# A fused attention and gated-MLP kernel: a persistent row of ones in the key-query tiles of the F32 heads, and a new instruction order

## The chip, the cores and the metric

The kernel runs on one core of one Trainium2 chip. The metric is the device time of one execution in microseconds (us). Before the change it is 783.78 us, the median of three runs (783.1 to 788.05).

## The reference

Attention with a bias from cumulative sums over 8 batches of 8 heads, 576 tokens of 64 dimensions, and behind it a gated MLP that mixes over tokens. Cut to what is computed:

```python
# attention, per batch and head: q, k, v are 576 x 64, s is 576
s_pos = np.maximum(s, 0.0)
cum = np.cumsum(s_pos, axis=-1)
bias = -(cum[:, :, :, None] - cum[:, :, None, :])
scores = np.where(causal, -1e9, q @ k.T / 8 + np.minimum(bias, 0.0))
attn = softmax(scores)                       # 1e-9 is added to the sum
x = (attn @ v).transpose(0, 2, 1, 3)         # 8 x 576 x 512
# MLP, per batch
h = gelu_tanh(x @ w_in)                      # 576 x 1024
u, v = h[..., :512], h[..., 512:]
v_n = (v - mean(v)) / sqrt(var(v) + 1e-6) * g_ln
v_s = einsum('ts,bsd->btd', w_sg, v_n) + b_sg[None, :, None]
out = x + (u * v_s) @ w_out
```

## The kernel before

**Work.** Each of the 64 heads passes three steps: `scores` (q times k with the cumulative sums as one extra row of the contraction, five query tiles `it` of 64 to 576 columns, then a masked minimum on VectorE, DVE below, and an exponential on ScalarE, ACT), `transposes` (twelve 128x128 transposes on TensorE, PE, into tiles `pa`, `pb`, `pd`) and `pv` (the product with v, tiles `xx` and, from head 16 on, `x0`, which the profile calls `x`). Eight heads are a batch, and `ffn` then runs the MLP of that batch while the next batch's heads go on. In the profile its PE groups are `vm`, `um`, `sm` and `om`.

**Precision.** Heads 0 to 11 (`h < NQ`) take q and k in plain F32, and heads 0 to 15 (`h < NP`) take v in plain F32. All later work is split into a high and a low F32R part, two or three matmuls each.

**The F32 heads' tile.** `kt` holds two tiles `kf` of 128 x 2 x 576, used in turn (`kt[h % 2]`). Rows 0 to 63 hold q in plane 0 and k in plane 1. Row 64 is the bias row: ones on the side of q, and head h's scaled cumulative sums, `cf[h]`, on the side of k. Rows 65 to 127 stay zero. The function `load` fills a tile with two transfers from the SP queue: `in_kf`, which in the kernel before brings 65 rows (row 64 with ones in plane 0 and zeros in plane 1), and, for h > 0, `cf[h]` into row 64 of plane 1. The second overwrites bytes of the first, so it waits until the first has landed, and SP issues its transfers strictly in order. Head 0 adds its bias with matmuls of their own (`sc<-cf,wz`).

**Order.** Nothing is issued where the code stands. Every operation is recorded with a key (`nc.key`, a place on the time axis of heads), a table `SHIFT` moves kinds of operations by some heads' time in each of five phases (`PHASE`), and `plan` schedules the recorded graph with the costs of `cost`, a latency per pair of engines plus `MARGIN` ns, and 280 bytes per ns for transfers. What comes out is one fixed sequence for each engine. All instructions therefore have one line in the profile, L418. `nc.gate` makes what is recorded under it start after another instruction has started.

**Start.** PE runs `WARM` matmuls on a constant tile (`wm<-wz`), then the cumulative sums (`cps`), which ACT and DVE bring to `cf`. GpSimd (POOL) clears the two `kf` tiles. The MLP weights arrive as 64-bit floats (`wraw`), and ACT, POOL and DVE turn them into two F32R parts (`wbits`, `wi`, `wo`), in the first 130 us, between the heads' work.

Of the kernel before, what the change touches and what calls it, by code (L numbers as in the profile page):

```python
# [17 lines left out]
B, H, S, D = 8, 8, 576, 64  # L18
# [3 lines left out]
P = 128  # L22
# [22 lines left out]
ORDL = ("v0 u00 v1 v2 u01 u02 v3 v4 u10 u11 s00 u12 u03 s01 s03 u13 s10 "  # L45
        "s02 o00 o01 s11 s12 s13 o03 o02 o11 o13 o10 o12")
CV = 1.4
WARM = 9
FULL = {(128, 192): 300.0, (128, 288): 525.0, (128, 320): 690.0, (128, 448): 830.0, (64, 64): 130.0, (128, 64): 200.0,
        (64, 128): 150.0, (64, 192): 215.0, (64, 256): 290.0}  # L50
NQ = 12
# [17 lines left out]
LATENCY = [[54, 38, 39, 80, 60], [54, 35, 33, 77, 60], [54, 34, 35, 90, 60], [55, 34, 35, 80, 60], [1060] * 5]  # L69
OVERLAP = [0, 93, 75, 25, 0]  # L70
YIELD = {DVE: 95, POOL: 60}
MARGIN = 58.3
ISSUE = 640.0
PHASE = (4.0, 9.0, 13.5, 61.5)
SHIFT = {
    "act activation p__ 128x192 p__": (4.33, 4.33, 4.33, 4.33, 4.33),
    "act activation p__ 128x320 p__": (-5.08, -5.08, -5.08, -5.08, -5.08),
    "act activation p__ 128x576 p__": (-3.57, -3.57, -3.57, -3.57, -3.57),
    "act activation p__ 64x64 p__": (0, 0, -2, 1.33, 0),
# [3 lines left out]
    "act copy k 128x576 raw": (0, 0, 0, 5.05, 0),  # L83
    "act copy pbh 128x256 pt": (6.99, 6.99, 6.99, 6.99, 6.99),
    "act copy pbh 64x128 pt": (0, 0, 0, 6.37, 6.37),
    "act copy pbl 128x128 pt": (2.4, 2.4, 2.4, 2.4, 0),
    "act copy pdh 128x256 pt": (0, 0, 0, -4.2, -4.2),
    "act copy vs 128x384 vr": (0, 0, 0, 1.69, 1.69),
    "act copy wi 128x256 wbits": (1.92, 1.92, 1.92, 0, 0),
# [5 lines left out]
    "dve scalar_tensor_tensor wbits 128x256 wraw": (0, 1.04, 0, 0, 0),  # L95
    "dve tensor_copy pbh 128x512 pt": (2.51, 2.51, 2.51, 2.51, 0),
    "dve tensor_copy pdh 128x256 pt": (0, 0, 0, -0.91, 0),
    "dve tensor_copy rt 10x128 pt": (-4.03, -4.03, -4.03, -4.03, -4.03),
    "dve tensor_scalar wbits 128x256 wbits": (0, 0, 6.16, 6.16, 0),
    "dve tensor_tensor pal 128x512 pt": (0, 0, 0, 3.87, 3.87),  # L100
    "dve tensor_tensor pbl 128x512 pt": (0, 0, 0, 0.91, 0.91),
    "dve tensor_tensor pdl 128x192 pt": (0, 0, 0, -1.48, -1.48),
    "dve tensor_tensor u 128x288 sm": (0, 0, 0, -0.43, -0.43),
    "dve tensor_tensor vm 64x512 vm": (0, 0, -2.45, 0, 0),
    "dve tensor_tensor_reduce p__ 128x192 sc": (-0.99, -0.99, -0.99, -0.99, -0.99),
    "dve tensor_tensor_reduce p__ 128x288 sc": (0, 1.63, 0, 0, 0),
    "dve tensor_tensor_reduce p__ 128x320 sc": (3.92, 3.92, 3.92, 3.92, 3.92),
    "dve tensor_tensor_reduce p__ 64x64 sc": (0, 0, 4.41, -23.41, 0),
# [23 lines left out]
    "pool tensor_scalar p__ 64x64 p__": (2.01, 2.01, 2.01, 2.01, 2.01),  # L132
    "pool tensor_scalar wbits 128x256 wbits": (0, 0, -7.72, 0, 0),
    "pool tensor_tensor gt 128x288 u": (0, 0, 0, 1.88, 1.88),
    "pool tensor_tensor k 128x576 raw": (0, 0, 0.53, 0, 0),
    "pool tensor_tensor wo 128x256 wbits": (0, 0, 19.65, 19.65, 0),
# [3 lines left out]
}  # L140


# [100 lines left out]
class Program:  # L243
# [30 lines left out]
    def cost(self, op):  # L274
        e, name, ins, outs, kw = op["eng"].n, op["name"], op["ins"], op["outs"], op["kw"]
        big = [v for v in ins if v.columns() > 1]
        n = outs[0].columns() if outs else big[0].columns()
# [3 lines left out]
        if e == PE:  # L281
            if name == "group":
                d, load = 2150.0, 54.0
            elif name == "transpose":
                d, load, port = 110.0, 0.84 * ins[0].columns(), 1.0
            else:
                w, m = ins
                load, n = 0.84 * w.columns(), m.columns()
                d = 0.463 * n if m.dtype == F32R else FULL.get((w.columns(), n), 2.0 * n + 60)
        elif e == ACT:  # L290
            f = kw.get("func")
            d = (195 if not any(ps) else 166) + 0.834 * n
            if f == AF.Exp:
                d, gap = 480 + 0.834 * n, -107
            elif n == 512 and f == AF.Copy:
                d = 715
            elif n == 384:
                gap = 115
            elif f == AF.Tanh:
                d += 10  # L300
        elif e == DVE:
            d = 150 + 1.045 * n
            if name == "scalar_tensor_tensor" and n == 512 and any(ps):
                d += 55
            if name == "tensor_tensor_reduce":
                d += 67 if isinstance(kw["scalar"], View) else 7
            elif name == "reciprocal":
                d = 202
            elif name == "bn_stats":
                d, gap = 687, 118  # L310
            elif name == "bn_aggr":
                d = 172
            elif name == "memset":
                d = 60 + 0.8 * n
            elif n > 1 and not ops_ and not any(ps):
                d = 152 + 1.04 * n if len(big) > 1 else 70 + 0.8 * n
                port = d
        elif e == POOL:
            if name == "tensor_tensor":
                d = (560 if kw["op"] == ALU.pow else 193) if n == 1 else 177 + 2.17 * n  # L320
            elif name == "tensor_scalar":
                d = 180 + (1.01 if n == 512 else 0.84) * n if n > 4 else 210
                if kw["op0"] == ALU.max:
                    d = 3.3 * n
            else:
                d = 140 + n
            if n > 4 and ins:
                port = min(d, 265.0) if kw.get("op0") == ALU.max else d
        else:
            v = (outs or big)[0]  # L330
            d, load = v.dims[0][1] * v.columns() * 4 / 280.0, ISSUE
        if e in (ACT, DVE) and any(v.off[1] for v in outs + big if v.columns() > 1):
            load, gap = 20.0, OVERLAP[e] + 25
        return e, d, load, port, gap
# [231 lines left out]
def tile_attn_gmlp(  # L566
# [45 lines left out]
    def load(h):  # L612
        d = heads[h] = {}
        if h < NQ:
            t = kt[h % 2]
            k = d["k"] = t[:, 1, :]
            d["q"] = t.rearrange("p a n -> p (a n)")
            r = D + (h > 0)
            nc.sync.dma_start(out=t[0:r], in_=kf[h, 0:r])
            if h:  # L620
                nc.sync.dma_start(out=k[D:D + 1, :], in_=cf[h:h + 1, :])
        else:
# [21 lines left out]
    for i in range(WARM):  # L644
# [8 lines left out]
    nc.gpsimd.memset(tri.bitcast(F32), 8.0)  # L653
    x = nc.gpsimd.affine_select(out=tri, in_=tri.bitcast(F32), pattern=[[1, S]], base=0, channel_multiplier=-1,
                                compare_op=ALU.is_ge, fill=0.0)
    nc.gate = x
    kt = []
    for i in range(2):
        t = att.tile([P, 2, S], F32, name="kf", tag="k1")
        kt_done = nc.gpsimd.memset(t[64:P].rearrange("p a n -> p (a n)"), 0.0)  # L660
        kt.append(t)
    nc.gate = None
    sp = moe.tile([P, 5, 2, BH], F32R, name="sp", tag="vn", bufs=4)
# [589 lines left out]
def _layout(i):  # L1253
# [5 lines left out]
    tok = (np.array(TOK)[:, None] * REM + np.arange(REM)).ravel()  # L1259
    kq = np.concatenate([k.transpose(0, 2, 1), q.transpose(0, 2, 1)[:, :, tok]], axis=1)  # L1260
    kf = kq[:NQ].reshape(NQ, 2, D, S)[:, ::-1].transpose(0, 2, 1, 3)
    row = np.zeros((NQ, 1, 2, S), q.dtype)
    row[:, :, 0] = 1
    kf = np.concatenate([kf, row], axis=1)
    v6 = np.concatenate([v, v[:, NT * P:], v[:, 0:REM], v[:, 0:REM]], axis=1)
    v6[:NP, NT * P:S] = 0
    v6[:NP, 5 * P + REM:] = 0
# [37 lines left out]
```

## Time and profile before

| what | us |
|---|---|
| median of three runs | 783.78 |
| lowest and highest run | 783.1, 788.05 |
| the profiled execution | 786.85 |
| its span, first to last instruction | 785.1 |
| busy in it: PE, DVE, ACT, POOL | 758.7, 602.5, 561.2, 499.3 |

The prediction reads the profile in views. A row of a list by time gives start, duration, engine, line, operation, output and inputs, and in brackets how long the engine stood idle before it and what ended that. SPq rows are transfers being issued by SP, not their flight. PEclk is the clock that PE was granted, 1.00 being full. In the chain of waits, which follows the last instruction back to what released it, a row gives start, duration and what ran.

### The profile page before, as it was taken

The numbers are of one execution on the slowest core, as the hardware profiler recorded it, in microseconds if no ns is written. First come the engines' busy times: TensorE is split into PE (matmuls) and PEld (weight loads), VectorE is DVE, ScalarE is ACT, GpSimd is POOL, SyncE is SP. The second block draws the span as 40 slices with busy tenths as digits, with TensorE's granted clock in tenths as the row PEclk, the third lists the DMA queues.
The fourth block names the chain that finished last, engine by engine and source line by source line (L and its number), as shares of the span: only waits on it lengthen the run. The fifth ranks groups of instructions, "written<-read, shape, count | busy, mean of one in ns | idle before, by whom it ended". The sixth has DMA issues, their size and how long they took to land.

```text
span 785.1 us, 16981 instructions
## 1 busy us (share of the span) xinstructions
PE 758.7 (97%) x5246; PEld 695.6 (89%) x5246; DVE 602.5 (77%) x1856; ACT 561.2 (71%) x1582; POOL 499.3 (64%) x820
## 2 busy tenths in 40 slices
PE   8998889999999999999999999999999999999998
PEld 6766668899899998999989998999989999899998
DVE  6678679866897769985899768987699858984662
ACT  4867867765888768885888758886688858871340
POOL 6557887774668565685567756684756856654541
PEclk9999999999999999999999999999999999999999
DMA  7547673553535625454344635356254544401101
GB/s 204 144 115 184 186 176 89 125 142 89 136 105 130 176 73 154 117 140 132 106 130 108 179 88 138 109 137 175 72 157 116 138 122 114 109 30 31 52 15 61
DMA packets 74119, 94.24 MB, mean 120 GB/s; under 512 B 29816, under 2 KB 44600, under 8 KB 74028
## 3 DMA queue, kind: packets, MB, share of 16 engines
q1 hardware_dynamic: 74028, 93.15, 44.7%
q8 instruction: 42, 0.69, 0.4%
q14 instruction: 49, 0.40, 0.2%
HBM read 49.38 MB, written 9.90 MB: 75 GB/s over the span
## 4 chain that ended last, share of the span: by engine, by line
PE 69%; DVE 10%; ACT 8%; DMA 4%; POOL 4%; issue 3%; SPq 1%; POOLq 0%; ACTq 0%; DVEq 0%
PE sm L418 12%; PE om L418 12%; PE sc L418 10%; PE vm L418 9%; PE xx L418 9%; PE um L418 9%; PE pt L418 7%; ACT p L418 3%; DVE u L418 1%; DVE p L418 1%; ACT k L418 1%; DVE pbl L418 1%; DVE xr L418 1%; DMA out_t<-ot 1%; DVE vt L418 1%
## 5 line engine op out<-in xcount | busy, mean ns | idle before, releaser
L418 ACT ACTIVATE p<-p,mn 128x192 f32<-128x192 f32 (+4 forms) x320 | 178.3, 558 | 36.3 <-DVE mn L418 34.0
L418 DVE CUSTOM_DVE_ANT_0 p<-sc,mask 128x288 f32<-128x288 f32 (+4 forms) x320 | 124.0, 421 | 9.1 <-PE sc L418 6.9
L418 PE MATMUL sm<-ws,vn 128*128 128x288 f32 x768 | 130.6, 300 | 0.2 <-DVE u L418 0.2
L418 PE MATMUL pt<-ident,p 128*128 128x128 f32 x768 | 120.7, 279 | 6.5 <-ACT p L418 5.0
L418 PE MATMUL om<-gt,wo 128*128 128x288 f32 x768 | 123.6, 299 | 0.0
L418 PE MATMUL um<-xs,wi 128*128 128x288 f32 x768 | 122.0, 301 | 0.0
L418 PE MATMUL vm<-wi,xs 128*128 128x512 f32 (+1 forms) x416 | 114.6, 401 | 0.0
L418 PEld LDWEIGHTS sm<-ws,vn 128*128 128x128 f32 x768 | 110.3, 189 | 1.9 <-DVE u L418 0.6
L418 PEld LDWEIGHTS om<-gt,wo 128*128 128x128 f32 x768 | 108.8, 188 | 1.2
L418 PEld LDWEIGHTS um<-xs,wi 128*128 128x128 f32 x768 | 106.7, 188 | 0.7
L418 PEld LDWEIGHTS pt<-ident,p 128*128 128x128 f32 x768 | 90.8, 141 | 17.0 <-ACT p L418 7.5
L418 PE MATMUL sc<-k 128*128 128x288 f32 (+4 forms) x312 | 87.4, 295 | 2.1 <-DVE vnr L418 0.8
L418 POOL TENSOR_TENSOR k<-raw,k 128x576 fp32r<-128x576 f32 x52 | 74.2, 1427 | 18.9 <-ACT k L418 18.6
L418 PEld LDWEIGHTS vm<-wi,xs 128*128 128x128 f32 (+1 forms) x416 | 73.8, 184 | 13.1
L418 PE MATMUL sc<-k,q 66*128 66x288 f32 (+4 forms) x312 | 80.5, 302 | 0.0
L418 POOL TENSOR_SCALAR p<-p 64x64 f32<-64x64 f32 x128 | 30.8, 240 | 69.1 <-ACT p L418 49.1
L418 DVE SCALAR_TENSOR_TENSOR u<-u,um 128x288 f32<-128x288 f32 x128 | 56.5, 448 | 17.4 <-ACT u L418 15.3
L418 DVE TENSOR_TENSOR pbl<-pt,pbh 128x512 fp32r<-128x512 f32 (+3 forms) x120 | 55.3, 469 | 17.0 <-ACT pbh L418 12.8
L418 POOL TENSOR_TENSOR gt<-u,gt 128x288 fp32r<-128x288 f32 x64 | 51.0, 807 | 22.7 <-ACT gt L418 22.7
L418 PEld LDWEIGHTS sc<-k 128*128 128x128 f32 (+1 forms) x312 | 55.4, 180 | 6.0 <-issue 1.2
L418 ACT ACTIVATION_READ_ACCUMULATOR p<-p,mn 128x1 f32 (+1 forms) x320 | 60.4, 189 | 0.0
L418 POOL TENSOR_TENSOR vs<-vr,vs 128x384 fp32r<-128x384 f32 x48 | 48.7, 1015 | 17.2 <-POOL p L418 8.9
(131 smaller groups left out, 1685.3 us busy)
## 6 DMA issues: line engine op xcount, KB each, us to landing
k<-k SPq DMA_DIRECT2D x156, 144.0 KB
raw<-in_kq SPq DMA_DIRECT2D x52, 288.0 KB
vr<-in_vp SPq DMA_DIRECT2D x48, 192.0 KB
rb<-rd SPq DMA_DIRECT2D x64, 144.0 KB
out_t<-ot SPq DMA_DIRECT2D x64, 144.0 KB
q<-k SPq DMA_DIRECT2D x52, 144.0 KB
wraw<-in_w_in SPq DMA_DIRECT2D x16, 256.0 KB
kf<-in_kf SPq DMA_DIRECT2D x11, 292.5 KB
```

What stands on the lines that cost most here:

```text
L418: real[i] = [getattr(op["eng"].real, name)(*[f(a) for a in args], **{k: f(v) for k, v in kw.items()}).ins for args, kw in calls]
```

## The change

Row 64 of the two tiles is no longer loaded. After the clearing of rows 64 to 127 a second memset writes ones into row 64 of plane 0, once, and `load` brings 64 rows. So the transfer of `cf[h]` shares no byte with the transfer of `in_kf`, and neither waits for the other. Both still wait until the matmuls of head h - 2 have read the tile. The first tile is now cleared by DVE, the second by POOL, and only the second one behind the gate. The host no longer appends the row.

The order is found anew: `SHIFT` is another table, `MARGIN` goes from 58.3 to 54.62 ns, transfers are planned at 235 bytes per ns, and there are ten `wm` matmuls.

```diff
-WARM = 9
+WARM = 10
...
-MARGIN = 58.3
+MARGIN = 54.62
...
-    "act activation p__ 128x192 p__": (4.33, 4.33, 4.33, 4.33, 4.33),
...
+    "act activation p__ 128x192 p__": (0, 0, 3, 3, 3),
...
-            d, load = v.dims[0][1] * v.columns() * 4 / 280.0, ISSUE
+            d, load = v.dims[0][1] * v.columns() * 4 / 235.0, ISSUE
...
-            r = D + (h > 0)
-            nc.sync.dma_start(out=t[0:r], in_=kf[h, 0:r])
+            nc.sync.dma_start(out=t[0:D], in_=kf[h])
             if h:
                 nc.sync.dma_start(out=k[D:D + 1, :], in_=cf[h:h + 1, :])
...
-    nc.gate = x
     kt = []
     for i in range(2):
         t = att.tile([P, 2, S], F32, name="kf", tag="k1")
-        kt_done = nc.gpsimd.memset(t[64:P].rearrange("p a n -> p (a n)"), 0.0)
+        e = (nc.vector, nc.gpsimd)[i]
+        nc.gate = x if i else None
+        kt_done = e.memset(t[64:P].rearrange("p a n -> p (a n)"), 0.0)
+        e.memset(t[64:65, 0, :], 1.0)
         kt.append(t)
...
-    row = np.zeros((NQ, 1, 2, S), q.dtype)
-    row[:, :, 0] = 1
-    kf = np.concatenate([kf, row], axis=1)
```

Three places show what the new order moves. The first is the SP queue at the start. `vr`, `raw`, `g_b` and `wraw` are loads for later, `cum` stores all cumulative sums for the heads from 12 on. Before, from the second head's load on:

```order
L418 DMA kf<-in_kf 65x1152
L418 DMA wraw<-in_w_in 128x512
L418 DMA g_b<-in_g_ln 128x512
L418 DMA raw<-in_kq 128x576
L418 DMA vr<-in_vp 128x384
L418 DMA kf<-cf 1x16x36
L418 DMA cum<-cc 64x2x576
L418 DMA wraw<-in_w_in 128x512
L418 DMA kf<-in_kf 65x1152
L418 DMA wraw<-in_w_in 128x512
L418 DMA kf<-cf 1x16x36
```

Now, from the first two heads' loads on:

```order
L431 DMA kf<-in_kf 64x1152 x2
L431 DMA wraw<-in_w_in 128x512 x2
L431 DMA vf<-in_vp 128x6x64
L431 DMA wraw<-in_w_in 128x512 x2
L431 DMA g_b<-in_g_ln 128x512
L431 DMA raw<-in_kq 128x576
L431 DMA vr<-in_vp 128x384
L431 DMA kf<-cf 1x16x36
L431 DMA cum<-cc 64x2x576
L431 DMA wraw<-in_w_in 128x512
L431 DMA kf<-cf 1x16x36
L431 DMA kf<-in_kf 64x1152
```

Head 1's load is ahead of all `wraw`, and from head 2 on the sums' transfer stands ahead of its own head's load instead of behind it.

The second is PE at heads 0 and 1. `p_3_103`, `p_2_80`, `p_1_214`, `p_4_223` are head 0's exponentials by query tile before, `p_3_94`, `p_2_78`, `p_1_217`, `p_4_203` are the same now, and `sc<-kf` are head 1's scores. Before, from head 0's transposes of query tile 2 on:

```order
L418 MATMUL pt<-ident,p_2_80 128x128 x2
L418 MATMUL pt<-ident,p_1_214 128x128
L418 MATMUL sc<-kf 128x448
L418 MATMUL sc<-kf 128x64
L418 MATMUL sc<-kf 128x320
L418 MATMUL pt<-ident,p_4_223 128x128 x3
L418 MATMUL pt<-ident,p_3_103 128x128
L418 MATMUL pt<-ident,p_4_223 128x128
L418 MATMUL pt<-ident,p_2_80 128x128
L418 MATMUL sc<-kf 128x192
L418 MATMUL sc<-kf 128x288 x2
L418 MATMUL pt<-ident,p_3_120 128x128
```

Now:

```order
L431 MATMUL pt<-ident,p_2_78 128x128 x2
L431 MATMUL pt<-ident,p_1_217 128x128
L431 MATMUL pt<-ident,p_4_203 128x128 x3
L431 MATMUL pt<-ident,p_3_94 128x128
L431 MATMUL pt<-ident,p_4_203 128x128
L431 MATMUL pt<-ident,p_2_78 128x128
L431 MATMUL sc<-kf 128x320
L431 MATMUL sc<-kf 128x192
L431 MATMUL sc<-kf 128x448
L431 MATMUL sc<-kf 128x64
L431 MATMUL sc<-kf 128x288 x2
L431 MATMUL xx<-pah,vf 64x256 x2
```

All transposes of head 0 come ahead of head 1's scores, and head 0's product follows those scores at once. Before, a transpose of head 1 (`p_3_120`) stood ahead of that product.

The third is PE at a head of a middle batch (head 30), between its last transpose and the products that read `pbh` and `pbl`, the split halves of transposed exponentials. Before, from the sixth of a run of `sm` to the first product that reads `pbh` (ahead of it, behind the last transpose, stand eleven `sm` and the `pah` and `pal` products):

```order
L418 MATMUL sc<-k_4600 128x448
L418 MATMUL sc<-k_4600 128x288
L418 MATMUL sc<-k_4606,q_0_167 128x288
L418 MATMUL sc<-k_4600 128x320
L418 MATMUL sc<-k_4606,q_0_167 128x320
L418 MATMUL sc<-k_4600 128x192
L418 MATMUL sc<-k_4606,q_0_167 128x192
L418 MATMUL sc<-k_4606,q_0_167 128x448
L418 MATMUL x_4831<-pdh,vs 128x64
L418 MATMUL sc<-k_4600 64x64
L418 MATMUL sc<-k_4606,q_0_167 64x64
L418 MATMUL xx<-pbh,vs 128x448
```

Now, from the last transpose on:

```order
L431 MATMUL pt<-ident,p_2_78 128x128
L431 MATMUL sm<-ws,vn 128x288 x5
L431 MATMUL xx<-pah,vs 128x512
L431 MATMUL xx<-pal,vs 128x512
L431 MATMUL sc<-k_4589 128x448
L431 MATMUL xx<-pbh,vs 128x448
L431 MATMUL sc<-k_4589 128x320
L431 MATMUL sc<-k_4593,q_0_165 128x320
L431 MATMUL sc<-k_4589 128x192
L431 MATMUL sc<-k_4593,q_0_165 128x192
L431 MATMUL xx<-pbl,vs 128x448
```

The product that reads `pbh` has moved up: 24 matmuls stood between it and the last transpose, now it is eight.

More of the change, by code (lines that the diff above doesn't have):

```diff
@@ L75 @@
 SHIFT = {
-    "act activation p__ 128x192 p__": (4.33, 4.33, 4.33, 4.33, 4.33),
-    "act activation p__ 128x320 p__": (-5.08, -5.08, -5.08, -5.08, -5.08),
-    "act activation p__ 128x576 p__": (-3.57, -3.57, -3.57, -3.57, -3.57),
-    "act activation p__ 64x64 p__": (0, 0, -2, 1.33, 0),
[3 rows of a table removed]
[L83 to L86, printed above, removed]
@@ L87 @@
-    "act copy pdh 128x256 pt": (0, 0, 0, -4.2, -4.2),
-    "act copy vs 128x384 vr": (0, 0, 0, 1.69, 1.69),
-    "act copy wi 128x256 wbits": (1.92, 1.92, 1.92, 0, 0),
[5 rows of a table removed]
[L95 to L107, printed above, removed]
@@ L108 @@
-    "dve tensor_tensor_reduce p__ 64x64 sc": (0, 0, 4.41, -23.41, 0),
[23 rows of a table removed]
[L132 to L136, printed above, removed]
[3 rows of a table removed]
+    "act activation p__ 128x192 p__": (0, 0, 3, 3, 3),
+    "act activation p__ 128x320 p__": (-2.775, -2.775, -2.775, -2.775, -2.775),
@@ new lines @@
+    "act activation p__ 128x448 p__": (0, 6.453, 0, 0, 0),
+    "act activation p__ 128x576 p__": (0, 0, 0, -3.286, 0),
+    "act activation p__ 64x64 p__": (0, 0, 0, 3.184, 0),
+    "act activation u 128x288 u": (0, 0, -4.195, -4.195, -4.195),
+    "act activation vt 128x512 vt": (0, 0, 6.005, 0, 0),
+    "act copy k 128x576 raw": (0, 0, 6.47, 6.47, 6.47),
+    "act copy pah 128x512 pt": (0, 0, 0, 2.092, 0),
+    "act copy pal 128x512 pt": (1.449, 1.449, 1.449, 1.449, 0),
+    "act copy pbh 128x512 pt": (0, 0, 0, 0.806, 0.806),
@@ new lines @@
+    "act copy pbh 64x128 pt": (0, 0, 0, 8.205, 8.205),
+    "act copy pdh 128x256 pt": (0, 0, 0, 0.9, 0.9),
+    "act copy vs 128x384 vr": (0, 0, 0, 1.886, 0),
+    "act copy wr 128x576 wst": (0, 0, 4.943, 0, 0),
[6 rows of a table added]
+    "dve scalar_tensor_tensor wbits 128x256 wraw": (0, -2.286, -2.286, -2.286, 0),
+    "dve scalar_tensor_tensor wm 128x256 wraw": (-1.159, -1.159, -1.159, 0, 0),
+    "dve tensor_copy rt 10x128 pt": (0, 0, 0, -1.802, 0),
+    "dve tensor_scalar vm 64x512 vm": (0, 0, 2.26, 2.26, 2.26),
@@ new lines @@
+    "dve tensor_scalar wm 128x256 wbits": (-1.07, -1.07, -1.07, 0, 0),
+    "dve tensor_tensor pal 128x512 pt": (0, 0, 0, 4.019, 4.019),
+    "dve tensor_tensor pdh 64x64 pt": (0, 0, 0, 0.898, 0.898),
+    "dve tensor_tensor xr 64x64 x": (0, 0, 0, 1.336, 1.336),
+    "dve tensor_tensor_reduce p__ 128x192 sc": (0, 0, -0.165, -0.835, 0),
+    "dve tensor_tensor_reduce p__ 128x288 sc": (0, 0, -0.73, 1.272, -1.904),
+    "dve tensor_tensor_reduce p__ 128x320 sc": (0, 5.172, 0, 4.841, 0),
+    "dve tensor_tensor_reduce p__ 64x64 sc": (0, 0, 0.987, -21.202, 0),
[28 rows of a table added]
@@ new lines @@
+    "pool memset pbl 64x128 -": (2.582, 2.582, 2.582, 2.582, 2.582),
+    "pool tensor_scalar bs 128x1 bs": (0, 0, 0, 2.619, 0),
+    "pool tensor_scalar p__ 64x64 p__": (0.826, 0.826, 0.826, 0.826, 0.826),
+    "pool tensor_scalar wbits 128x256 wbits": (-11.991, -11.991, -11.991, -11.991, 0),
+    "pool tensor_scalar xs 128x576 xr": (0, 0, -6.829, 0, 0),
+    "pool tensor_tensor k 128x576 raw": (0, 0, 0, -1.271, 0),
+    "pool tensor_tensor vs 128x384 vr": (0, 0, 0, -1.162, -1.162),
+    "pool tensor_tensor wo 128x256 wbits": (0, 0, 15.613, 15.613, 0),
@@ L140 @@
+    "pool tensor_tensor wr 1x576 wst": (0, 0, 0.652, 0, 0),
+    "pool tensor_tensor ws 128x576 wst": (0, 0, -0.681, 0, 0),
[6 rows of a table added]
 }
```

74 rows, old and new, of the table SHIFT are left out of this document.

## The prediction

> **What bounds the kernel now.** I read the page first, then the windows by stage, then PE's rows and the chain of waits where a stage loses time. The page says that PE is busy nearly all the time and carries most of the chain.
>
> ```profile
> span 785.1 us, 16981 instructions
> PE 758.7 (97%) x5246; PEld 695.6 (89%) x5246; DVE 602.5 (77%) x1856; ACT 561.2 (71%) x1582; POOL 499.3 (64%) x820
> ```
>
> The windows (stretch, length, then busy time of PE, PEld, DVE, ACT, POOL, granted clock, share of the transfer engines, GB/s) show where it is not:
>
> ```profile
> 0.00:30.00 30.00, 25.52 (x126) 19.13 (x128) 19.60 (x72) 16.68 (x52) 17.39 (x34) 0.94 0.67 173
> 30.00:60.00 30.00, 28.22 (x195) 21.91 (x194) 23.34 (x86) 22.45 (x74) 16.79 (x28) 0.94 0.50 135
> 60.00:90.00 30.00, 26.51 (x177) 19.66 (x175) 21.70 (x83) 22.59 (x71) 23.17 (x31) 0.94 0.71 189
> 90.00:150.00 60.00, 54.35 (x388) 45.49 (x387) 51.02 (x147) 46.33 (x134) 48.09 (x77) 1.00 0.56 134
> 150.00:700.00 550.00, 543.30 (x3808) 511.95 (x3808) 445.21 (x1383) 427.25 (x1197) 356.53 (x588) 1.00 0.46 124
> 700.00:785.20 85.20, 80.83 (x564) 77.45 (x562) 41.68 (x92) 25.91 (x59) 37.35 (x65) 1.00 0.12 37
> ```
>
> PE's idle time is 4.5, 1.8, 3.5, 5.7, 6.7 and 4.4 us. So 550 us of middle batches can give 6.7 at most, the first 150 us up to 15.5, and 1.95 of those lie ahead of PE's first matmul (its row stands below), where this order changes nothing. The first 90 us also have a clock below full. PE's waits there:
>
> ```profile
> 21.06 0.47 PE L418 MATMUL pt<-ident,p 128*128 128x128 f32 x1 [2.31 <-ACT p L418]
> 50.48 2.29 PE L418 MATMUL sc<-kf 128*128 128x448 f32 x6 [1.78 <-DMA kf<-cf]
> 64.69 1.75 PE L418 MATMUL sc<-kf 128*128 128x448 f32 x6 [0.67 <-DVE wm L418]
> 69.08 0.44 PE L418 MATMUL pt<-ident,p 128*128 128x128 f32 x2 [0.43 <-POOL p L418]
> 71.19 1.02 PE L418 MATMUL sc<-kf 128*128 128x448 f32 x2 [1.35 <-DVE mn L418]
> ```
>
> I call them A (2.31 us), B (1.78) and C (0.67, 0.43, 1.35, together 2.45). Each costs more than its idle time. The chain of waits has equal work behind them and elsewhere:
>
> ```profile
> 13.96 5.32 DMA wraw<-in_w_in
> ...
> 21.53 3.06 PE xx L418 x16
> ...
> 28.75 1.67 PE xx L418 x16
> ...
> 42.72 1.71 PE sc L418 x6
> 44.43 1.00 PE pt L418 x9
> 45.77 4.67 DMA kf<-cf
> 50.48 2.29 PE sc L418 x6
> 52.77 1.93 PE pt L418 x9
> ...
> 72.21 3.18 PE xx L418 x16
> ```
>
> Behind A sixteen `xx` take 3.06 instead of 1.67, 1.39 more. Behind B the scores and transposes take 2.29 + 1.93 instead of 1.71 + 1.00, 1.51 more. Behind C `xx` takes 1.51 more. So A costs 3.70 us, B 3.29, C 3.96. The clock says why:
>
> ```profile
> 20.00:24.00 4.00, 2.94 (x17) 2.16 (x19) 1.30 (x5) 3.96 (x14) 2.25 (x4) 0.61 0.32 91
> 52.00:56.00 4.00, 4.00 (x17) 3.32 (x16) 2.11 (x9) 2.44 (x8) 1.73 (x3) 0.62 0.05 15
> ```
>
> It falls to 0.61 and 0.62 for about 4 us after 2.31 and 1.78 us of idle. [...]
>
> **Where the change bears: SP.** SP issues in order, and the sums' transfer waited for the load. SP's list of waits (total, times, longest) and its rows by time:
>
> ```profile
> SPq L418 <- DMA kf<-in_kf: 13.9, 7, 4.5
> ...
> 12.50 0.60 SPq L418 DMA_DIRECT2D kf<-cf  x1
> ...
> 13.96 0.55 SPq L418 DMA_DIRECT2D wraw<-in_w_in  x1
> ...
> 41.29 0.31 SPq L418 DMA_DIRECT2D kf<-in_kf  x1
> ```
>
> SP stood 13.9 us in seven such waits, 4.5 at the longest. Those waits go.
>
> *B.* Head 6's load is issued at 41.29, its sums only at 45.77, behind three other transfers that the old order put between, and they land 4.67 us later (the chain above), 9.2 us after the load's issue. Now the sums go first and both fly together, so the tile is ready after one flight of about 4.7 us, and SP is past no wait of the load. I take all of B, 3.3. Bounds: 0, if another transfer is late instead, and 3.3.
>
> *A.* PE waited for exponentials of head 1, and ACT stood behind a weight tile whose transfer came late. That row, and rows of the start that the next steps use:
>
> ```profile
> 19.30 0.43 ACT L418 ACTIVATE wbits<-wraw 128x256 f32<-128x256 f32 x1 [3.06 <-DMA wraw<-in_w_in]
> 13.33 0.65 PE L418 MATMUL sc<-cf,wz 128*128 128x288 f32 x2
> 14.58 0.78 ACT L418 ACTIVATE p<-p,mn 128x576 f32<-128x576 f32 x1
> 1.95 4.21 PE L418 MATMUL wm<-wz 128*128 128x512 f32 x9 [1.95 <-DVE wz L418]
> 2.21 2.05 POOL L418 MEMSET kf<- 64x1152 f32 x2
> 2.22 0.54 DVE L418 MEMSET cf<- 64x576 f32 x1 [0.18 <-issue]
> 3.12 0.49 DVE L418 TENSOR_SCALAR sp<-st 128x320 fp32r<-128x320 f32 x1
> ```
>
> That transfer was issued at 13.96 because head 1's sums held SP until 12.50. Now the sums wait for `cf` alone, and the weight tile can be issued about 1.2 us earlier; ACT also has head 0's copies ahead of that tile, so it waits less. A goes: 3.7. But a new wait opens. Head 0's last scores ended at 13.98 and its widest exponential at 15.36, 1.4 us later. Nine matmuls (three of them F32 scores, long) stood in between on PE; the new order has six transposes there, 0.67 us at 1.00 for nine. So PE idles some 0.7 us. Net 3.0. Bounds: 0 and 3.7.
>
> *Warm-up and memsets.* A tenth `wm` is 4.21 / 9 = 0.47 us on PE; an 0.18 us wait for the first load lay behind it. I take +0.3, bounds 0 and 0.5. DVE takes over one clearing (1.05 on POOL) and a memset of 576 columns (0.54, as `cf`), ahead of `sp`, which then ends at about 5.5 us instead of 4.1. PE's tenth `wm` ends at 6.6 and covers it; uncovered, 1.4 us would fall on the sums that follow. POOL loses one clearing and gains one short memset ahead of masks that nobody waits for yet. The 65th row of eleven loads is 1.5% of their bytes: nothing. [...]
>
> *C and the rest of the start.* Between 60 and 90 us DVE and POOL do weights, `xs` and heads (21.70 and 23.17 us of 30, 51.02 and 48.09 of the next 60), and two of C's waits are for DVE, one for POOL. That work is not less. In the F32 heads the new order puts more PE work between a score and its transpose: for heads 4 to 8 5.7 to 8.7 us (query tile 2) against 4.9 to 5.5, counted in the order at the prices of the chain's rows (1.71 for three pieces of scores, which the profile counts as six, 1.00 for nine transposes, 1.67 for a head's `xx`); but for heads 9 to 12, where C lies, about the same. I take 1.5 of C, bounds 0 and 4.0. For 90 to 150 us I take 0, bounds 2 either way.
>
> *Middle batches.* No transfer there depends on the persistent row; only the order moves. From the list of PE's waits, PE's rows, the chain, and the tiles `pbh` and `pbl` (minimum, median and maximum in ns, first and last start) in the stretch 209.5 to 212.2:
>
> ```profile
> PE x L418 <- DVE pdh L418: 4.7, 6, 0.8
> ...
> 209.60 0.60 PE L418 MATMUL pt<-ident,p 128*128 128x128 f32 x4
> ...
> 199.71 2.80 PE vm L418 x12
> ...
> L418 ACT CAST pbh<-pt x2: 270/430/589, 210.0 to 210.5; 128x512 fp32r<-128x512 f32 x1, 128x128 fp32r<-128x128 f32 x1
> L418 DVE TENSOR_TENSOR pbl<-pt,pbh x2: 275/476/678, 211.0 to 211.6; 128x512 fp32r<-128x512 f32 x1, 128x128 fp32r<-128x128 f32 x1
> ```
>
> From the end of four transposes (210.2) to both halves of `pb` takes 0.6 and 1.7 us (210.8 and 211.9). PE needs 0.455 ns per column (2.80 / 12 / 512). By that price the least work between a head's last transpose and its `pbh` product is 2.9 us before and 0.9 now, up to `pbl` 3.7 before and 1.6 now. The `x` product, which loses 0.8 us once per batch with 3.4 us behind the transposes, has 2.6 to 3.5 at several heads now. So old waits may go, and tight places are added. I take +1.5 us. Bounds: -6.7, all idle time gone, and +14.4, three such waits of 0.8 at each of six batches. At the end I take 0, bounds 1 either way.
>
> **The sum.** -3.3 - 3.0 + 0.3 - 1.5 + 1.5 = -6.0 us. The profiled execution took 786.85 with a span of 785.1, 3.07 over the median of 783.78; it would become 780.85, and the median 777.8.
>
> **Rivals.**
> *All waits of the start go* (faster): A 3.0, B 3.3, C 4.0, 2.0 in 90 to 150 us, and 1.0 in the middle; with the warm-up 13.0, so 770.8. For it: SP no longer stands. Against it: POOL's and DVE's work between 60 and 120 us stays.
> *The transfers' waits only move* (the change doesn't do what it says): the engines of the transfers ran at 0.67 and 0.71 of their time there, and an early load delays the weight tiles behind it. A and B return under other names, C gives 1.0, the middle costs 1.5: 784.6. Against it: 4.5 us of B's delay was order, not bandwidth.
> *Tight evacuations in the middle* (slower): the three places per batch above cost their 14.4 us against 7.5 won at the start: 790.7. It outweighs the gain from 1.6 waits of 0.8 per batch on. For it: the margins of 0.9 and 1.6 us against 0.6 and 1.7 needed. Against it: ACT and DVE are reordered with PE, and PE's whole idle time there is 6.7 us over six batches, 1.1 per batch.
> [...]
>
> **How the numbers follow.** Chances: forecast 0.42, all go 0.23, moved 0.19, tight places 0.10, clock 0.06. One per cent, about what a measurement of this kernel can tell from no change, is 7.8 us: below 776.0, above 791.6. All of "all go" and a sixth of the forecast's own spread (774 to 782) are faster, 0.30; half of "tight places" is slower, 0.05; 0.65 stays within. The range, 770.5 to 787, leaves out the upper part of "tight places" and the edge of "all go".
>
> **What would show it.** No wait of SP for `in_kf` ahead of the sums, and no wait of PE for `kf<-cf`; full clock from 24 to 60 us; a short wait at head 0's wide transposes near 15 us; the first `xx` near 19 to 20 us instead of 21.5. In the middle, PE idle per batch near 1.4 us. It would be wrong if PE waits there for `pbl` or `pdh` at several heads per batch, or if new waits of 1.5 us and more with clock dips appear before 90 us.

## The result and the profile after

The changed kernel takes 794.54 us (median of five runs, 792.70 to 795.65) against 783.78 before: 1.0116 times the time, with a 95% interval of 1.0081 to 1.0152. It is slower by a little over 1%. The forecast was 777.8, within 770.5 to 787.

The page's head and first part for the changed kernel:

```profile
span 792.8 us, 16977 instructions
...
PE 765.9 (97%) x5247; PEld 696.1 (88%) x5247; DVE 601.0 (76%) x1858; ACT 563.9 (71%) x1582; POOL 498.6 (63%) x820
...
PE 60%; ACT 12%; DVE 12%; issue 5%; DMA 4%; POOL 4%; SPq 0%; POOLq 0%; DVEq 0%; ACTq 0%
```

The third line is the chain's share by engine. PE is 97% busy as before, so the page's first part hides the loss. What shows it is the chain: it runs through ACT and DVE for 24% of the span, where the same line of before has 18%:

```profile
PE 69%; DVE 10%; ACT 8%; DMA 4%; POOL 4%; issue 3%; SPq 1%; POOLq 0%; ACTq 0%; DVEq 0%
```

The windows of the changed kernel (columns as in the prediction):

```profile
0.00:30.00 30.00, 27.17 (x133) 19.86 (x135) 23.68 (x84) 18.68 (x57) 17.62 (x37) 1.00 0.70 184
30.00:60.00 30.00, 27.44 (x202) 20.89 (x201) 23.91 (x91) 23.37 (x82) 18.99 (x31) 1.00 0.58 143
60.00:90.00 30.00, 26.58 (x167) 19.58 (x168) 21.12 (x76) 21.58 (x67) 23.29 (x29) 0.94 0.71 176
90.00:150.00 60.00, 55.79 (x403) 47.34 (x400) 49.48 (x139) 45.10 (x130) 46.82 (x79) 0.97 0.55 138
150.00:700.00 550.00, 539.68 (x3725) 503.03 (x3723) 432.95 (x1354) 420.68 (x1165) 350.67 (x576) 1.00 0.47 122
```

The first 60 us now have full clock, 1.00; from 60 to 150 us it is below, 0.94 and 0.97. PE's idle time from 150 to 700 us is 10.3 us, 6.7 before. That stretch holds fixed times, not fixed work: it counts 3725 rows of PE where it counted 3808. For fixed work I use two markers that every profile has in its chain of waits, the start of the sixteen `om` of the first and of the sixth batch. Of before, then of after:

```profile
189.53 2.12 PE om L418 x16
...
646.45 2.12 PE om L418 x16
```

```profile
186.02 2.12 PE om L431 x16
...
653.91 2.12 PE om L431 x16
```

The work up to the first marker takes 186.02 instead of 189.53 (3.5 less), the five batches between them, called the middle below, 467.89 instead of 456.92 (11.0 more), and the rest to the end of the span 0.2 more. Since the profiled execution of before was 3.07 over its median and the one of after is the median, 11.0 + 0.2 - 3.5 + 3.07 makes the 10.8 us between the medians. So the loss is the middle, and the gain at the start is one against a slow execution of before.

PE's waits over 0.2 us from 190 to 650 us (total, times, longest), of before and of after:

```profile
PE x L418 <- DVE pdh L418: 3.9, 5, 0.8
PE xx L418 <- DVE pbl L418: 1.6, 5, 0.3
PE pt L418 <- DVE xr L418: 0.3, 1, 0.3
```

```profile
PE xx L431 <- ACT pbh L431: 3.4, 5, 0.8
PE x L431 <- DVE pdh L431: 3.3, 5, 0.7
PE xx L431 <- DVE pdh L431: 1.5, 2, 0.7
PE sm L431 <- DMA vnr<-vnr: 0.4, 1, 0.4
PE sc L431 <- DMA k<-k: 0.3, 1, 0.3
```

The named waits add up to 5.8 and 8.9. That is 3 of the 11 us; the rest does not stand in this view. The windows from marker to marker, of before and of after, say where it is:

```profile
189.53:646.45 456.92, 451.06 (x3162) 426.29 (x3162) 373.40 (x1160) 357.55 (x1000) 298.75 (x492) 1.00 0.47 127
```

```profile
186.02:653.91 467.89, 458.56 (x3159) 427.11 (x3159) 371.01 (x1160) 360.39 (x999) 298.36 (x489) 1.00 0.48 124
```

PE's idle time (length less busy time) grew from 5.9 to 9.3 us, and its busy time by 7.5 us, for the same matmuls but for three rows, at full clock. So 7.5 of the 11 us are time that the profile counts as busy.

At the start, PE's rows of the changed kernel with a wait, and the clock behind two of them:

```profile
14.86 0.77 PE L431 MATMUL pt<-ident,p 128*128 128x128 f32 x3 [0.26 <-ACT p L431]
16.05 0.88 PE L431 MATMUL pt<-ident,p 128*128 128x128 f32 x6 [0.43 <-ACT p L431]
...
19.67 0.65 PE L431 MATMUL xx<-pah,vf 128*64 128x256 f32 x4
...
52.83 0.51 PE L431 MATMUL sc<-kf 128*128 128x288 f32 x1 [1.59 <-DVE wbits L431]
...
70.95 0.55 PE L431 MATMUL xx<-pbl,vf 128*64 128x256 f32 x3 [1.97 <-ACT pbl L431]
...
98.86 0.33 PE L431 MATMUL pt<-ident,p 128*128 128x128 f32 x1 [2.73 <-ACT xr L431]
```

```profile
72.00:76.00 4.00, 4.00 (x21) 3.50 (x18) 2.40 (x8) 3.37 (x12) 4.00 (x5) 0.57 0.57 139
100.00:104.00 4.00, 4.00 (x14) 2.78 (x14) 2.68 (x7) 1.64 (x6) 2.25 (x6) 0.62 0.84 233
```

A and B are gone, SP hardly stands for `in_kf` (total, times, longest; 13.9 us in seven waits before),

```profile
SPq L431 <- DMA kf<-in_kf: 1.1, 2, 0.8
```

the first `xx` starts at 19.67, and three other waits have come, two of them with the slow clock behind them.

### The profile page after: what moved, and what is told of

It reads as the page before. It is cut to its first block, busy times and chain, and to the rows that moved or that the text cites. A ratio compares the mean times of both kernels' runs of the same rounds, so it can differ in the third digit from the quotient of the medians.

```text
span 792.8 us, 16977 instructions
## 1 busy us (share of the span) xinstructions
PE 765.9 (97%) x5247; PEld 696.1 (88%) x5247; DVE 601.0 (76%) x1858; ACT 563.9 (71%) x1582; POOL 498.6 (63%) x820
## 4 chain that ended last, share of the span: by engine, by line
PE 60%; ACT 12%; DVE 12%; issue 5%; DMA 4%; POOL 4%; SPq 0%; POOLq 0%; DVEq 0%; ACTq 0%
PE sm L431 13%; PE om L431 10%; PE sc L431 9%; PE vm L431 8%; PE xx L431 7%; PE um L431 7%; PE pt L431 6%; ACT p L431 4%; DVE p L431 3%; DVE pbl L431 2%; DVE u L431 1%; DMA k<-k 1%; ACT pbh L431 1%; ACT xr L431 1%; DVE xr L431 1%
## 5 line engine op out<-in xcount | busy, mean ns | idle before, releaser
L431 ACT ACTIVATE p<-p,mn 128x320 f32<-128x320 f32 (+4 forms) x320 | 177.9, 557 | 28.0 <-DVE mn L431 26.0
L431 DVE CUSTOM_DVE_ANT_0 p<-sc,mask 128x320 f32<-128x320 f32 (+4 forms) x320 | 124.7, 420 | 15.5 <-PE sc L431 10.1
L431 PE MATMUL sm<-ws,vn 128*128 128x288 f32 x768 | 133.1, 301 | 0.0
L431 PE MATMUL vm<-wi,xs 128*128 128x512 f32 (+1 forms) x416 | 112.1, 404 | 0.0
L431 PE MATMUL sc<-k 128*128 128x288 f32 (+4 forms) x312 | 90.2, 299 | 1.4 <-DMA k<-k 1.0
L431 PE MATMUL sc<-k,q 66*128 66x288 f32 (+4 forms) x312 | 83.2, 301 | 0.0
L431 DVE TENSOR_TENSOR pbl<-pt,pbh 128x512 fp32r<-128x512 f32 (+3 forms) x120 | 54.7, 467 | 22.4 <-ACT pbh L431 14.4
L431 ACT CAST pbh<-pt 128x512 fp32r<-128x512 f32 (+3 forms) x120 | 48.4, 410 | 17.3 <-DVE rt L431 5.9
```

What stands on the lines that cost most here:

```text
L431: real[i] = [getattr(op["eng"].real, name)(*[f(a) for a in args], **{k: f(v) for k, v in kw.items()}).ins for args, kw in calls]
```

## The experiments

Theory 1: the new order of the middle brings PE's products too close behind the evacuations that they need. Rivals: the row, its memsets and its transfers cost the time themselves (2); the start's other state is carried on into the middle (3); the middle's loss lies elsewhere, in scores, transfers or the sequence of matmuls (4). All results stand in one table; the first marker and the middle are from each run's chain of waits, in us.

| run | first marker | middle | median (runs) | ratio to before, 95% |
|---|---|---|---|---|
| before | 189.53 | 456.92 | 783.78 (5) | |
| after | 186.02 | 467.89 | 794.54 (5) | 1.0116, 1.0081 to 1.0152 |
| `row_alone` | 183.28 | 456.16 | 779.98 (6) | 0.9936, 0.9913 to 0.9958 |
| `row_replan` | 193.66 | 456.52 | 791.18 (6) | 1.0088, 1.0063 to 1.0113 |
| `start_new` | 185.63 | 456.67 | 783.89 (12) | 1.0002, 0.9980 to 1.0023 |
| `start_old` | 191.76 | 465.44 | 798.51 (5) | 1.0182, 1.0153 to 1.0211 |
| `mid_pe` | 185.17 | 471.78 | 797.60 (4) | 1.0178, 1.0138 to 1.0219 |
| `mid_rest` | 188.17 | 476.32 | 805.41 (4) | 1.0275, 1.0239 to 1.0311 |
| `after_free` | 184.82 | 464.65 | 789.95 (7) | 1.0084, 1.0062 to 1.0106 |
| `before_free` | 186.76 | 455.46 | 781.35 (8) | 0.9957, 0.9934 to 0.9980 |
| `after_narrow` | 186.53 | 447.90 | 772.54 (2) | 0.9851, 0.9675 to 1.0026 |
| `before_narrow` | 184.13 | 447.54 | 770.79 (2) | 0.9828, 0.9625 to 1.0031 |
| `after_narrow_b` | 185.90 | 449.95 | 773.25 (2) | 0.9860, 0.9731 to 0.9988 |
| `after_narrow_ad` | 184.88 | 453.92 | 776.75 (8) | 0.9904, 0.9885 to 0.9924 |
| `row_first` | 185.34 | 457.14 | 781.05 (12) | 0.9952, 0.9937 to 0.9968 |

The runs of before beside the experiments had medians of 783.29 to 784.12 where there were nine or more of them.

### The row without the order

`row_alone` has the persistent row, but `plan` is given the dependences and costs of before, so that it finds the old sequence:

```diff
+    was = [set(p) for p in pre]
+    for a, b in nc.pairs:
+        was[b].add(a)
...
+    _, _, _, seqs = plan(cost, was, new, uses, order, bufs, prio, after)
```

> The persistent row and the 64-row loads in the order of before: every engine runs the sequence of before, with two short memsets of ones on POOL added. Measured by two markers in the chain of waits, the start of the sixteen om of the first and of the sixth batch (before 189.5 and 456.9 us later, now 186.0 and 467.9 later). Theory 1, the new order of the middle makes evacuations tight: middle stays at 457 (1 either way), the wait of PE for kf<-cf near 50 us goes, the start is 0 to 3.5 us shorter, the time 780 to 784. Rival 2, the row itself, its memsets or the two transfers in flight at once cost the time: middle 463 or more, or a start longer than 189.5, and a time of 788 and more.

The middle is that of before and the time is 0.64% lower, just under the band expected. Rival 2 falls: the row costs nothing and, by itself, gains 3.3 us. The mechanism was not the expected one, though: the wait B is still there. Head 0's first `xx`, PE's two longest waits between 20 and 100 us, and the clock behind them:

```profile
19.31 0.65 PE L419 MATMUL xx<-pah,vf 128*64 128x256 f32 x4
...
47.51 1.78 PE L419 MATMUL sc<-kf 128*128 128x448 f32 x6 [2.01 <-DMA kf<-cf]
...
66.62 1.02 PE L419 MATMUL sc<-kf 128*128 128x448 f32 x2 [1.25 <-DVE mn L419]
```

```profile
48.00:52.00 4.00, 4.00 (x26) 3.05 (x26) 2.75 (x10) 2.31 (x9) 3.25 (x6) 1.00 0.21 61
68.00:72.00 4.00, 4.00 (x38) 3.46 (x33) 3.15 (x11) 3.59 (x11) 3.78 (x6) 1.00 0.89 229
```

What went is A (that `xx` started at 21.53 before), and the slow clock: all six runs have a mean granted clock of 1.000, while 17 runs of before beside them have 0.993 to 1.000 and 780.32 to 788.21 us.

`row_replan` keeps the whole code change and takes back only the numbers (`SHIFT`, `MARGIN` 58.3, 280 bytes per ns, nine `wm`):

> The whole change but for the numbers that make the order: table, margin, rate of transfers and nine wm as before, planned again. From a third of the program on the sequence of every engine is that of before. Theory 1: middle 457, time 778 to 785, depending on what the planner makes of the start. Rival 2 (the row itself costs): 788 and more. Rival 3 (what the start does differently is carried into the middle, by buffers and transfers that come at other times): middle 460 or more.

Middle 456.5, so rival 3 falls here. The start is 4 us longer than before and the time is 6 us above the expected band: with the new dependences the old numbers give a start in which one score waits 4.96 us:

```profile
71.77 1.09 PE L418 MATMUL sc<-kf 128*128 128x448 f32 x1 [4.96 <-DMA kf<-cf]
```

So new numbers were needed for the start, and the row's gain is there only with an order that fits.

### Start and middle apart

Both runs have the persistent row. `start_new` takes phases 0 to 2 of the table (recorded up to head 13.5) from the change and phases 3 and 4 from before, with `MARGIN` and the rate of transfers switched at the same place; `start_old` is the reverse.

```diff
-MARGIN = 54.62
+MARGIN = (54.62, 58.3)
+RATE = (235, 280)
+CUT = 13.5
```

> The whole change, but the table, margin and rate of before for everything recorded from head 13.5 on: the start in the new order, the middle in the order of before. Theory 1: start as now, about 186, middle 457, time 779 to 782, faster than both. Rival 3 (the start's new order lengthens the middle): middle 462 or more, time 786 and more.

> The reverse: table, margin, rate and warm-up of before up to head 13.5, those of the change from there on, the row persistent throughout. The middle runs in the new order. Theory 1: middle 466 to 469, time 789 to 797, slower by over 1%. Rival 3: middle near 457, time 780 to 785.

The middle follows its own numbers, whatever the start: 456.7 with the old ones, 465.4 with the new (0.6 under the expected band; the time is 1.5 over it, since the old numbers lose more at the start). Between the markers `start_new` runs the sequence of before on PE, ACT and DVE, row for row by tile and shape, behind another start, and takes as long: rival 3 falls for good. The middle of `start_old` is near the changed kernel's sequence and not the same, so the 2.4 us between their middles stay open. `start_new` was expected faster than both and is as fast as before; the new start is 3.9 us slower than the old sequence of `row_alone` with the same row. By medians the change thus splits into the row (-3.3), the start's new order (+3.9, 779.98 to 783.89) and the new order of the middle and the end (+10.7, 783.89 to 794.54).

### Which part of the table

The start of the change throughout; in the middle, `mid_pe` takes only the new entries on PE operations, `mid_rest` only those on all others; `MARGIN` and the rate of transfers are there those of before. Two of the entries by which `mid_pe` differs from `start_new`:

```diff
-    "pe matmul om 128x288 wo": (0, 0, 0, 2.24, 2.24),
+    "pe matmul om 128x288 wo": (0, 0, 0, 2.707, 2.707),
...
-    "pe matmul sc 128x288 k": (0, 0, -0.634, -3.64, -3.64),
+    "pe matmul sc 128x288 k": (0, 0, -0.634, -0.634, -0.634),
```

> Start in the new order, middle (recorded from head 13.5 on) by the numbers of before, but for the table's entries on PE operations, which are the new ones. Theory 1, with PE's new places as the cause: the middle takes 462 to 468, since evacuations stay where they were and the products come closer behind them. If the evacuations' new places are the cause: 457 to 460. With the order of before it took 456.7.

> The reverse: in the middle the table's entries on ACT, DVE, POOL and SP operations are the new ones, those on PE and the margin and the rate of transfers those of before. Evacuations' new places as the cause: 462 to 468. PE's new places as the cause: 457 to 460. Both above 460: the order of before is a tuned whole, and any part of another table loses it.

Each half alone loses more than the whole: 471.8 and 476.3, both above their expected 462 to 468. Only the last case named for `mid_rest`, both above 460, came true. The wait that grows most is the same in both, that of `xx` for ACT's `pbh`, 3.4 us in the changed kernel and not in the list of before (total, times, longest, 190 to 650 us, `mid_pe` and then `mid_rest`):

```profile
PE xx L437 <- ACT pbh L437: 10.0, 10, 1.3
```

```profile
PE xx L434 <- ACT pbh L434: 9.5, 5, 1.9
```

So PE's places and those of the other engines do not share the blame in parts that add up.

### Is it the evacuations?

`after_free` and `before_free` keep each engine's sequence, and let the products of the heads from 16 on read a weight tile, so that no product waits for an evacuation; the output of those heads is left out:

```diff
+            if op["eng"].n == PE and op["name"] == "matmul" and op["args"][2].buf.name in ('pah', 'pal', 'pbh', 'pbl', 'pdh', 'pdl'):
+                op["args"] = (*op["args"][:2], free[:, 0, 0, 0:op["args"][2].columns()])
```

> The changed kernel, order unchanged, but the products of the heads from 16 on read a constant weight tile in place of the transposed exponentials pah, pal, pbh, pbl, pdh and pdl: their output is left out, the evacuations still run, and no product waits for one. Markers are the starts of the sixteen om of the first and sixth batch (changed kernel 467.9 us apart, before 456.9). Theory 1 (the new order brings products too close behind their evacuations): the middle falls to 450 to 457, and is within 3 us of the same edit in the kernel before. Rival 4 (the 11 us are from elsewhere: scores waiting for k and q, the MLP's small matmuls, PSUM buffers, contention): the middle stays at 460 or more and 8 us or more above the same edit in the kernel before.

> Control: the same edit in the kernel before, order unchanged; the products of the heads from 16 on read a constant weight tile, so the outputs of those heads are left out. Theory 1: the middle falls from 456.9 by 2 to 7 us, to 450 to 455, since its waits for pdh and pbl add to 6.3. Rival 4: as little change as in the changed kernel.

This spoke against theory 1 as I had put it: the middles fall by 3.2 and 1.5 and stay 9.2 apart, as rival 4 has it. But the waits of `after_free` show that they had moved (190 to 650 us):

```profile
PE pt L434 <- DVE xr L434: 2.8, 6, 0.5
PE pt L434 <- DVE pdh L434: 2.0, 5, 0.6
```

Now transposes wait. The tiles `pt`, `xx` and `x0` turn in three PSUM buffers, and a transpose can start only when DVE and ACT have emptied the oldest. The same evacuation holds PE at its next user. So the edit was too small, and `after_narrow` and `before_narrow` add that the evacuations themselves become short from head 17 on, at their old place in the sequence:

```diff
+            if op["eng"].n in (ACT, DVE) and op["key"] > 17 and op["outs"][0].buf.name in ('pah', 'pal', 'pbh', 'pbl', 'pdh', 'pdl'):
+                cut = 72 if op["outs"][0].columns() == 256 and op["outs"][0].buf.name == "pdh" else 8
+                f = lambda x: x.make()[..., 0:cut] if isinstance(x, View) else x
```

> The changed kernel, order unchanged; as in the run that freed the products, the products of the heads from 16 on read a weight tile, and from head 17 on the evacuations of the transposes on ACT and DVE move 8 columns (one of them 72) in place of up to 512, so they take little time but stand where they stood: the output of those heads is left out. Theory 1 in its wider form (evacuations end too late in the new order; freed of them, the products hand the wait to the next transposes, which need the same PSUM banks): the middle falls from 467.9 (464.7 with free products) to 452 to 456, within 2 us of the same edit in the kernel before. Rival 4 (scores, transfers, or the sequence of matmuls itself): it stays 5 us or more above the same edit in the kernel before.

> Control: the same edit in the kernel before. Theory 1: the middle goes from 456.9 (455.5 with free products) to 451 to 455. Rival 4: the same, and it is the changed kernel that stays above.

The middles become equal: 447.90 and 447.54. The windows of `after_narrow` and of `before_narrow`:

```profile
150.00:700.00 550.00, 549.71 (x3889) 522.21 (x3888) 384.43 (x1403) 386.41 (x1206) 366.37 (x598) 1.00 0.47 124
```

```profile
150.00:700.00 550.00, 549.82 (x3887) 523.08 (x3887) 383.49 (x1399) 380.95 (x1202) 364.19 (x595) 1.00 0.46 123
```

Both middles come out below what was expected, and PE is idle for less than 0.3 of the 550 us. The two sequences of PE are worth the same, and rival 4 falls. What full-length evacuations cost PE is 456.92 - 447.54 = 9.4 us in the order of before and 467.89 - 447.90 = 20.0 in the new one: the 11 us but for 0.4. Between the markers 5.9 of the 9.4 are idle time of PE, and 9.1 of the 20.0; the profile counts the rest as busy. The edit also takes work from ACT and DVE (42 and 57 us between the markers of the changed kernel), so it shows that the loss comes through these two engines, whose work is the same in both kernels and only its order differs. That it is the evacuations, and not other work freed behind them, is argued from the list of waits, where 8.2 of the 8.9 us are for `pbh` and `pdh`.

The last pair makes the same edit on `pbh` and `pbl` alone, and on the other four tiles alone.

> The changed kernel, order unchanged, with the edit on the tiles pbh and pbl alone: their products in the heads from 16 on read a weight tile, their evacuations from head 17 on move 8 columns, so the output of those heads is left out. The edit on all six tiles took the middle from 467.9 to 447.9. If the places that the order shows as tight (last transpose to the products of pbh and pbl) are where the 11 us are lost: the middle falls to 455 to 460, that is by 8 to 13. If the loss is spread over all evacuations: by 3 to 7, to 461 to 465.

> The complement: the same edit on pah, pal, pdh and pdl alone, the output of the heads from 16 on left out. Loss at pbh and pbl: the middle falls by 4 to 9 only, to 459 to 464, since 20.0 us in all go when both edits are made. Loss spread: by 10 to 17, to 451 to 458.

The middle falls by 17.9, more than either case expected, and by 14.0, within the band for a loss that is spread. That is 31.9 together where both edits give 20.0, so the loss can't be shared out by tile. The likely reason, not tested by itself: evacuations stand in one queue on ACT and one on DVE, and shortening any of them lets the rest come earlier. A place of the changed kernel shows the queue, PE's rows and then ACT's:

```profile
248.14 0.60 PE L431 MATMUL pt<-ident,p 128*128 128x128 f32 x4
...
252.07 0.44 PE L431 MATMUL xx<-pbh,vs 128*128 128x448 f32 x1 [0.77 <-ACT pbh L431]
```

```profile
250.53 0.59 ACT L431 CAST pdh<-pt 64x64 fp32r<-64x64 f32 x2 [1.45 <-DVE pbl L431]
251.02 0.67 ACT L431 ACTIVATE p<-p,mn 128x448 f32<-128x448 f32 x1
251.59 0.19 ACT L431 ACTIVATION_READ_ACCUMULATOR p<-p,mn 128x1 f32 x1
251.68 0.24 ACT L431 CAST pbh<-pt 64x128 fp32r<-64x128 f32 x1
```

The transposes end at 248.74. ACT waits 1.45 us for DVE's `pbl`, then casts `pdh`, then runs an exponential of a later head, and casts the last piece of `pbh` only then, ending at 251.92: 3.2 us behind the transposes, and PE has 2.6 us of other work. Over the heads of the middle (40 of them in rows, the product's start less the end of its last cast) that product starts within 0.4 us of the cast at 10 heads before and at 18 now. The casts themselves do not come later: the last one ends 1.2 to 3.3 us behind the head's transposes before (median 2.6) and 0.4 to 3.2 now (median 1.5). The products have come closer to them.

### The sums ahead of the load

`row_first` is `row_alone` with one edit in SP's sequence: for heads 2 to 11 the transfer of the sums goes directly ahead of its own head's load.

```diff
+    for a, b in nc.pairs[2:]:
+        seqs[SP].remove(b)
+        seqs[SP].insert(seqs[SP].index(a), b)
```

> The persistent row in the order of before, with one edit in SP's queue alone: for heads 2 to 11 the sums' transfer stands directly ahead of its own head's load, not behind the transfers that the old order put between (the queue order that the change has). With the row alone PE still waited 2.0 us for kf<-cf at 47.5, that transfer being issued at 42.5 and the load at 38.1. Theory 1 (what held the sums was their place in the queue, so B goes): no wait of PE for kf<-cf of over 0.5 us, the first marker at 180.5 to 182.5 in place of 183.3, middle 456 to 457, time 777 to 779.5, ratio 0.990 to 0.994. Rival (the transfers' waits only move, since flight and bandwidth set them): a wait of 1.5 us or more for kf<-in_kf or a weight tile in the same place, first marker 183 to 185, time 779.5 to 782.

PE's scores now start at 45.67 without a wait, so the place in the queue had set B. The time is not lower: the ratio of 0.9952 lies inside the interval of `row_alone`, above its 0.9936. Two pieces of this run's chain, the scores, and one of the two waits behind which the clock falls in the profiled run (the slowest of the twelve, 782.89, with a mean clock of 0.996):

```profile
40.48 5.48 DMA wraw<-in_w_in
...
46.32 1.85 ACT p L419 x6
```

```profile
45.67 1.78 PE L419 MATMUL sc<-kf 128*128 128x448 f32 x6
...
67.09 1.41 PE L419 MATMUL sc<-kf 128*128 128x448 f32 x2 [1.00 <-DVE mn L419]
```

The chain now passes through a weight tile's transfer, which lands at 46.0 us, and through DVE and ACT behind it. Six of the twelve runs have a mean clock below 1.000; the other six take 779.93 to 780.96, no less than `row_alone`, so the clock does not hide a gain. In the time the forecast's rival, that the transfers' waits only move, is what happened to B; its sign, a wait of PE of 1.5 us or more in the same place, is not there (the longest from 30 to 60 us is 0.54). `row_alone` is the fastest version found that computes the whole output, 0.64% below before and 1.8% below the change (779.98 against 794.54).

## Why the prediction was wrong

**Middle batches, +1.5: this step failed.** It was right that the persistent row does nothing there and that the new order makes places tight; it measured +11.0. The error lay in the price. I took what an evacuation needs, 0.6 us up to `pbh`, from the rows of 209.5 to 212.2 us of before, and compared it with PE's 0.9 us. That stretch ends ahead of this head's third cast of `pbh`, which the same product reads:

```profile
212.88 0.26 ACT L418 CAST pbh<-pt 64x128 fp32r<-64x128 f32 x1 [0.43 <-DVE pdl L418]
```

It ends at 213.14, 2.9 us behind the transposes and not 0.6; over the 40 heads the need was 1.2 to 3.3 us already before. So PE's 0.9 us had no margin of 0.3; by this need it could fall short by up to 2.4. I had named the number that decides, PE's least work behind the last transpose, and had counted it on PE alone, for two tiles; its counterpart, what stands ahead of the last cast on ACT and DVE, was in the order too. I had also held PE's small idle time, 1.1 us per batch, against such losses, while evacuations cost 9.4 us in five batches even before, 3.5 of it counted as busy. PE's idle time between the markers is 1.9 us per batch now, 1.4 forecast.

**The rival "tight evacuations in the middle" is what came.** Priced at 14.4, measured 11.0; with the start's 3.5 it is slower, as it said. Its three waits of 0.8 us per batch are not what the list shows: there are twelve waits for `pbh` and `pdh` in five batches (ten for `pdh` and `pbl` before), and most of the loss is counted as busy. Its chance of 0.10 was too low. The argument against it, that ACT and DVE are reordered with PE, was no measurement: the casts do end sooner behind the transposes, but the products moved up too. Of the other rivals, that all waits of the start go fell with the three new waits. The 0.06 for the clock, that it slows down whatever these waits are, the runs do not decide: it fell behind a wait of 1.97 to 1.99 us in eight profiles of eight, behind one of 2.72 to 2.74 in six, and behind one of 1.59 in none.

**A, -3.7 + 0.7: right.** Head 0's product starts at 19.67 (forecast 19 to 20), the new wait is 0.26 + 0.43 = 0.69, and the clock is full from 20 to 60 us.

**B, -3.3: right on its cause, wrong on its worth.** No wait for `kf<-cf` is left, and `row_first` shows that the queue was the reason. But where that wait was, a score now waits 1.59 us for DVE's `wbits` (52.83), and `row_first` gained nothing without it.

**C, -1.5: wrong.** In its place PE waits 1.97 us for `pbl`, with the slow clock behind it, which the forecast had named as a sign of being wrong.

**90 to 150 us, 0 within 2: not measured by itself.** PE's idle time there fell from 5.7 to 4.2 us, in spite of a wait of 2.73 us at 98.86, but the mean clock of 0.97 is 1.8 us of 60.

**Warm-up +0.3, end 0:** the end measured +0.2; the tenth `wm` was not measured by itself.

**The base.** The sum was made against an execution with three stretches of slow clock (0.61, 0.62 and 0.57 in the 4 us from 20, 52 and 72 us), 3.07 us over the median, and I subtracted that difference at the end as if it were spread. Two of the three stretches were in A and B: against the median a part of both was not there to be won. In `before_free` and `before_narrow`, which start as before does, A is a wait of 2.10 and 2.34 us, and the clock stays at 1.00 behind it. So the 1.39 us of clock in A's price belong to some executions only.

## What to carry to other kernels

Where a change brings a new dependence and a newly found order together, take them apart by giving the planner the old dependence: here the first was worth -0.64% and the second more than ate it. Before trusting a new order, count for every consumer how long ahead of it the last piece of its producer ends, on the producer's engine and over all repetitions, because PE's busy time can hide the loss: 7.5 of 11 us here. And where an edit removes one wait and the time stays, look at the next user of the same buffer before dropping the theory.

## What the hardware showed

The slow clock is not a fixed price of a wait. Eight profiles share the first part of the changed order (the changed kernel, `start_new`, and the six runs that change only heads behind them), and with it three waits of PE: 1.59 us near 52 us, 1.97 to 1.99 near 71, 2.72 to 2.74 near 98. Behind the first the clock never falls (1.00 from 53 to 57 us in the changed kernel), behind the second in all eight (0.57 from 72 to 76 us in the changed kernel and in `start_new`), behind the longest in six of eight. `start_new` is one of the two where it doesn't, with a mean clock of 0.998 where the six have 0.994 to 0.996; the row and its window:

```profile
98.14 0.33 PE L438 MATMUL pt<-ident,p 128*128 128x128 f32 x1 [2.73 <-ACT xr L438]
```

```profile
100.00:104.00 4.00, 4.00 (x32) 2.97 (x31) 3.10 (x8) 2.74 (x8) 2.73 (x9) 1.00 0.73 208
```

Both falls of the changed kernel cost the same: 0.43 of 4 us at 72 to 76, and at 100 to 104 0.38 with 0.05 in the 4 us ahead, are 1.7 us each. The 17 runs of before beside `row_alone` spread over 780.32 to 788.21 us as their mean clock goes from 1.000 to 0.993.
